# Gate sums and the first value projections as 128-column matmuls, and two admission settings of the planner, in a two-branch attention kernel

## The chip, the cores and the metric

The kernel runs on one core of a Trainium2 chip. The metric is the device time of one execution in microseconds (us). Lower is better. Four runs of the kernel before are given, and their median is what a changed kernel is compared with.

## The reference, cut to what matters

The input x has 2048 rows (tokens) of 512 features. Everything is in bf16 at the interface.

```python
g = sigmoid((x * gate_w).sum(-1, keepdims=True))      # one number per token
a = full attention of x, 32 heads of 16, then @ A_wo  # softmax(q k^T / 4) v
b = windowed attention of x: each token sees itself and 7 earlier ones,
    two apart, 32 heads of 16, then @ B_wo
return g * a + (1 - g) * b
```

The full attention (branch A) is by far the larger part: 32 heads times 2048 x 2048 scores have to be exponentiated. Branch B has only eight scores for each token and head.

## The kernel before, in words

**Units.** The scores of branch A are made in units. A unit is one head, 128 keys (the partitions) and 512 queries (the free axis). Four heads make a group (`NG` = 8 groups), 512 queries a chunk (`NC` = 4 chunks), and one pair of chunk and group is a *period*: 32 periods of 4 x 16 = 64 units, 2048 units in all. Four heads lie in four 32-row strips of the TensorE array, so several score matmuls (`kt_all` as weights, `qt` streaming) can run at the same time.

**Three ways for a unit to be exponentiated.** Most units are written into two PSUM rings, A with three banks and B with two. ScalarE (ACT) reads a whole ring with one activation (`pT<-ring`, 128x1536 or 128x1024) while TensorE fills the other ring. Other units go to a spare PSUM bank (`w0` or `w1`). From there VectorE (DVE) computes the exponential as a cubic in four passes (`ta`, `ta`, `ta`, `pd`), or GpSimd (POOL) does so after a copy (`psc`). Such a unit is called a rider when it is issued beside a ring fill. The result of each unit is multiplied by the values (`vp_all` as weights, 17 columns: 16 values and a one that sums the denominators) into one accumulator bank, `acc`.

**The other work** goes through the same two spare banks `w0` and `w1`, as *jobs*: the projections of keys (`k_job`, `kpk_job`), queries (`q_job`, `qpk_job`) and values (`v_job`, `v_group`), the gate sums (`g_job`), the transposes after each period (`post_job`, `ot_job`), branch B (`b_proj`, `b_attn`, most of it on POOL), and the output projections (`final_job`, two blocks of four matmuls).

**Order.** A planner (class `Plan`, lines 52 to 289) decides at build time in which order each engine gets its instructions. It keeps an assumed duration for each step and a list of ready steps for each engine. The hardware then executes each engine's list in that order and waits on semaphores where data is missing. The parts of it that the change touches:

- `fits` (line 216) lets a job with priority 2 or more onto PE only if it ends before ACT would run out of work. The tolerated overrun grows by `RAMP` (line 182) for each microsecond that the job has waited beyond `CALM` = 4.
- `JW` (line 190) is used twice. In `room_for_job` (line 200) a job that needs a spare bank is admitted once DVE's planned backlog is at least `JW`, or after it has waited `JP` = 3. In `rider` (line 1068) a further rider is refused if DVE's backlog is at least `JW` and a job waits for a bank.
- `have` and `idle_fill` (lines 144 to 168) count how much of the last 3.4133 us PE streamed, and put filler matmuls (`z32` as weights, results that are zero) where that falls under a share of 0.80. `P.thin` tells the count how much of a step's assumed duration is not streaming.

**The places of the change.** `gw` (line 365) holds the gate vector as four columns. `g_job` (lines 781 to 805) makes for each of 16 token tiles one column of 16 sums, by four matmuls with one streamed column each, in four steps of 16 matmuls. `v_group(0, 4, ...)` (line 1577) makes the values of the first four heads, needed by the first period: eight token tiles share a bank, 64 columns each. `v_group(4, 8, ...)` (line 1584) makes those of the next four heads for the third period. `v_group(8, 16, ...)` makes eight heads at a time with four token tiles in a bank, so 128 columns each.

## Time and profile before

| What | Value |
|---|---|
| Median of 4 runs | 860.02 us (855.65, 859.66, 860.39, 861.17) |
| The profiled execution | 860.39 us, of which span of instructions 858.6 us |
| ACT busy | 832.5 us (97%) |
| PE busy | 758.6 us (88%) |
| DVE busy | 749.5 us (87%) |
| POOL busy | 735.1 us (86%) |
| Mean granted TensorE clock | 0.983 |
| First and last `pT` activation | starts at 18.67 us, ends at 849.15 us |

The profile is one execution. "Busy" is the time in which an engine had at least one instruction in work, and matmuls are pipelined, so a busy PE is not PE at its peak. A *group* is all instructions of the same engine, operation and tiles, with their count, total busy time and mean duration. A group's durations can add up to more than its busy time, since neighbouring activations or matmuls overlap. The *timeline* lists instructions in order of time, merged where nothing came between, with the idle time of the engine before them in brackets and what ended it. In the *windows* view each line is a stretch of time with every engine's busy time and the granted clock of TensorE. Nearly all instructions carry line 347, that of a helper, so tiles are used to tell them apart. A number of an activation in the order of rings (ring 0 is the first) is used for places: rings follow each other every 1.13 us or so.

### The profile page before, as it was taken

The page shows a single profiled execution, that of the slowest core. Times are in us where ns is not written, and L with a number is a line of the kernel's source. Part 1 is how long each engine was busy: PE and PEld are TensorE (multiplying, and loading weights), DVE is VectorE, ACT ScalarE, POOL GpSimd, SP SyncE. Part 2 cuts the span into 40 slices and gives each one's busy share as a digit, 9 for nine tenths or more (in the row PEclk, how much of TensorE's full clock was granted, in tenths as well). Part 3 has the DMA queues.
Part 4 walks back from the last instruction along what each step waited for, and adds up shares of the span by engine and source line. Part 5 has one row for each costly group of instructions (what it writes and reads, how often), then busy time and mean ns, then how long its engine had stood idle before and what let it go on. Part 6 is the DMA issues. An engine that isn't in the chain of part 4 may idle for free.

```text
span 858.6 us, 15867 instructions
## 1 busy us (share of the span) xinstructions
PE 758.6 (88%) x5935; PEld 268.7 (31%) x5935; DVE 749.5 (87%) x1314; ACT 832.5 (97%) x753; POOL 735.1 (86%) x740
## 2 busy tenths in 40 slices
PE   8999999888898898888889899988888989888897
PEld 4333343333233222323233233332322332222232
DVE  4488989899899889889999988899889998899896
ACT  4899999999999999999999999999999999999996
POOL 2576798999898999898999998989999998978871
PEclk9799999999999989999999999999999999799999
DMA  9001233412314231121030314213003203010000
GB/s 294 2 2 49 81 113 117 134 62 76 117 44 136 90 107 68 51 67 50 8 111 31 100 37 141 75 56 111 1 14 117 74 21 122 20 50 7 1 2 26
DMA packets 55727, 59.78 MB, mean 70 GB/s; under 512 B 3665, under 2 KB 52305, under 8 KB 55649
## 3 DMA queue, kind: packets, MB, share of 16 engines
q1 hardware_dynamic: 54304, 58.37, 21.2%
q8 instruction: 46, 0.75, 0.4%
q10 hardware_dynamic: 1344, 0.39, 0.2%
q14 instruction: 33, 0.26, 0.1%
HBM read 46.14 MB, written 12.62 MB: 68 GB/s over the span
## 4 chain that ended last, share of the span: by engine, by line
ACT 66%; issue 21%; PE 11%; DVE 1%; POOL 0%; ACTq 0%
ACT pT L347 65%; PE acc L347 4%; PE ring L347 3%; PE w L347 3%; ACT lg L347 1%; DVE ta L347 1%; PE s L347 1%; PE e L347 0%; POOL prod L347 0%; DVE absq L347 0%; DVE kpk L347 0%; POOL lg L347 0%; ACT osc L347 0%; DVE accS L347 0%; DVE pd L347 0%
## 5 line engine op out<-in xcount | busy, mean ns | idle before, releaser
L347 ACT ACTIVATE pT<-ring 128x1536 bf16<-128x1536 f32 x722 | 822.3, 1386 | 9.6 <-PE ring L347 5.6
L347 PE MATMUL ring<-qt,kt_all 32*128 32x512 bf16 x1849 | 290.3, 385 | 89.9 <-ACT pT L347 75.1
L347 DVE SCALAR_TENSOR_TENSOR ta<-ta,w 128x512 f32<-128x512 f32 x450 | 301.8, 682 | 6.5
L347 POOL TENSOR_TENSOR prod<-prod 128x512 f32<-128x512 f32 (+1 forms) x208 | 240.4, 1167 | 6.0
L347 PE MATMUL acc<-pT,vp_all 128*17 128x512 bf16 x1804 | 228.7, 388 | 3.0 <-DVE accS L347 2.2
L347 PEld LDWEIGHTS <-kt_all 32*128 32x128 bf16 x2093 | 112.4, 91 | 334.2 <-issue 317.2
L347 DVE TENSOR_SCALAR ta<-w 128x512 f32<-128x512 uint16 x225 | 153.4, 685 | 41.9 <-PE w L347 39.5
L347 PE MATMUL acc<-ident,z 128*17 128x512 bf16 (+5 forms) x660 | 166.2, 337 | 1.4 <-DVE wkp L347 1.4
L347 DVE SCALAR_TENSOR_TENSOR pd<-ta,w 128x512 uint16<-128x512 f32 x225 | 151.6, 677 | 1.8
L347 POOL TENSOR_TENSOR prod<-ksh,qb 128x512 f32<-128x512 bf16 x128 | 145.1, 1157 | 2.4
L347 POOL TENSOR_TENSOR prod<-vsh,lg 128x512 f32<-128x512 bf16 x128 | 136.7, 1099 | 2.5
L347 PE MATMUL w<-qt,kt_all 32*128 32x512 bf16 x244 | 93.2, 387 | 0.2 <-DVE pd L347 0.2
L347 PE MATMUL acc<-pd,vp_all 128*17 128x512 bf16 x244 | 80.1, 387 | 0.0
L347 PEld LDWEIGHTS <-vp_all 128*17 128x17 bf16 x2048 | 42.0, 88 | 98.1 <-issue 97.6
L347 POOL TENSOR_TENSOR psc<-psc 128x512 f32<-128x512 f32 x57 | 68.1, 1194 | 4.4
L347 PEld LDWEIGHTS <-z 128*17 128x17 bf16 (+1 forms) x666 | 46.4, 92 | 64.8 <-issue 44.8
L347 POOL TENSOR_SCALAR psc<-psc 128x512 f32<-128x512 uint16 (+1 forms) x38 | 23.6, 621 | 42.1 <-DVE psc L347 34.4
L347 PE MATMUL w<-bw,xT 128*128 128x512 bf16 x192 | 49.7, 381 | 0.3
L347 PEld LDWEIGHTS <-xT 128*128 128x128 bf16 x512 | 30.8, 98 | 30.0 <-issue 17.1
L347 POOL TENSOR_TENSOR lg<-lg,mx 128x256 f32<-128x256 f32 x16 | 10.1, 630 | 25.8 <-DVE mx L347 23.7
L347 DVE CAST kvs<-w 128x512 bf16<-128x512 f32 x32 | 21.8, 682 | 4.1 <-PE w L347 4.1
L347 DVE COPY accS<-acc 128x512 f32<-128x512 f32 (+1 forms) x32 | 21.6, 676 | 2.8 <-ACT accS L347 2.0
(112 smaller groups left out, 487.5 us busy)
## 6 DMA issues: line engine op xcount, KB each, us to landing
ksh<-kv_scr SPq DMA_DIRECT2D x16, 1024.0 KB
vsh<-kv_scr SPq DMA_DIRECT2D x16, 1024.0 KB
kv_scr<-kvs SPq DMA_DIRECT2D x16, 256.0 KB
kt_all<-k_scr SPq DMA_DIRECT2D x6, 512.0 KB
q_scr<-qpk SPq DMA_DIRECT2D x24, 128.0 KB
qt<-q_scr SPq DMA_DIRECT2D x24, 128.0 KB
out_dram<-osb SPq DMA_DIRECT2D x14, 128.0 KB
xr<-in_A_x_dram SPq DMA_DIRECT2D x3, 512.0 KB
```

The source lines that it names most:

```text
L347: return chain_on(self._key, f(*a, **k))
```

## The change

```diff
-    RAMP = 0.02
+    RAMP = 0.01
...
-    JW = 1.6
+    JW = 1.2
...
-    gw = const.tile([128, DC], BF16, name="gw")
+    gw = work.tile([128, DC, 128], BF16, name="gw", tag="qpk", bufs=2)
...
-    with nc.allow_non_contiguous_dma(reason="tiny gate vector load"):
-        A.dma_start(out=gw[:], in_=gate_w.rearrange("(c p) -> p c", p=128))
...
     V.memset(z32[:], 0.0)
+    V.memset(gw[:].rearrange("p c n -> p (c n)").bitcast(U32), 0)
     V.memset(warm[:], 0.0)
+    with nc.allow_non_contiguous_dma(reason="tiny gate vector load"):
+        A.dma_start(out=gw[:, :, 0], in_=gate_w.rearrange("(c p) -> p c", p=128))
     A.activation(out=warm[:], in_=warm[:], func=ACT.Exp)
...
-                    w.open(s, [128, NT])
+                    w.open(s, [128, NT + 127])
+                P.thin = 0.06
                 for t in range(t0, t0 + 4):
-                    P.thin = 0.65
                     for c in range(DC):
-                        mm(w.t[:, t:t + 1], xT[:, c, t * 128:(t + 1) * 128], gw[:, c:c + 1], c == 0, c == DC - 1)
+                        mm(w.t[:, t:t + 128], xT[:, c, t * 128:(t + 1) * 128], gw[:, c, :], c == 0, c == DC - 1)
...
-            yield ("pe", prio, 0.8, pe(t0)) + (("w",) if t0 == 0 else ())
+            yield ("pe", prio, 0.99, pe(t0)) + (("w",) if t0 == 0 else ())
...
-        yield ("act", -1, 0.3, lambda: A.activation(out=e1[:], in_=w.t[:], func=ACT.Exp, scale=-1.0))
+        yield ("act", -1, 0.3, lambda: A.activation(out=e1[:], in_=w.t[:, 0:NT], func=ACT.Exp, scale=-1.0))
...
-    v_group(0, 4, None, 3)
+    v_group(0, 8, None, 3)
...
-    v_group(4, 8, ev_start[0], due(2) + 0.1)
```

The gate vector is now the first of 128 columns, of which the other 127 are zero. The tile takes one of the two buffers of the tag `qpk` instead of its own, is cleared by VectorE, and is loaded by ScalarE's DMA queue after that. A gate matmul streams 128 columns and writes column t of the bank and zeros into the next 127, which the following tiles overwrite. The values of heads 0 to 7 are made together by what was already the path for eight heads: four passes of four token tiles, each of 16 matmuls with 128 columns, in place of two plus two passes of eight tiles with 64 columns. `RAMP` and `JW` change the planner's admission of jobs, and so the order of PE's and DVE's lists through the whole kernel.

## The prediction

> **What bounds the kernel now.** I read the page first: the engine line, the granted clock by slices, and the two largest groups with their shapes kept apart.

> ```profile
> PE 758.6 (88%) x5935; PEld 268.7 (31%) x5935; DVE 749.5 (87%) x1314; ACT 832.5 (97%) x753; POOL 735.1 (86%) x740
> ...
> PEclk9799999999999989999999999999999999799999
> ```
> ```profile
> L347 ACT ACTIVATE pT<-ring 128x1536 bf16<-128x1536 f32 x361 | 577.4, 1600 | 8.2 <-PE ring L347 5.6 <-PE w L347 1.7 <-PE acc L347 0.2
> L347 ACT ACTIVATE pT<-ring 128x1024 bf16<-128x1024 f32 x360 | 422.8, 1175 | 1.3 <-PE w L347 0.9
> ```

> ACT is the bound, nearly without a pause. The reader sees 361 activations of three units, 360 of two (and one of one unit), and 8.2 + 1.3 = 9.5 us of idle time before them. The 2nd, 15th and 35th of the 40 slices (21.5 us each) have a low clock. The undisturbed rate comes from the chain of waits:

> ```profile
> 134.30 1.24 ACT pT L347
> 135.54 0.10 issue
> 135.64 0.87 ACT pT L347
> 136.51 0.04 issue
> 136.56 1.25 ACT pT L347
> ```

> A pair (five units) takes 136.56 - 134.30 = 2.26 us. The two of a pair sum to 1.600 + 1.175, so 0.51 us of overlap per pair, 0.26 per activation, is lost as well wherever ACT has to pause. The floor of the stream is 361 x 2.26 = 815.9, plus 0.8 for the last single unit, plus branch B's 16 softmax activations at 0.30 each (143.33 to 143.63 in the timeline), 4.7: together 821.4 us. It really ran from 18.67 to 849.15, 830.5 us. So 9.1 us are stalls, and no reordering can win more. Where are they? The timeline of ACT shows most of the idle time in one place:

> ```profile
> 33.32 2.36 ACT L347 ACTIVATE pT<-ring 128x1536 bf16<-128x1536 f32 x2 [0.72 <-PE ring L347]
> 36.93 1.45 ACT L347 ACTIVATE pT<-ring 128x1536 bf16<-128x1536 f32 x1 [1.24 <-PE ring L347]
> ...
> 41.62 1.02 ACT L347 ACTIVATE pT<-ring 128x1024 bf16<-128x1024 f32 x1 [0.69 <-PE w L347]
> 42.82 2.36 ACT L347 ACTIVATE pT<-ring 128x1536 bf16<-128x1536 f32 x2 [0.17 <-PE ring L347]
> ...
> 672.52 15.93 ACT L347 ACTIVATE pT<-ring 128x1536 bf16<-128x1536 f32 x14 [0.49 <-PE w L347]
> ```

> The windows view says why. These are three stretches, cut where the clock changes:

> ```profile
> 30.94:41.18 10.24, 10.24 (x72) 2.63 (x71) 5.96 (x8) 7.92 (x8) 9.40 (x11) 0.50 0.00 0
> 310.83:317.66 6.83, 6.82 (x35) 2.06 (x35) 4.89 (x11) 6.24 (x7) 6.20 (x8) 0.50 0.75 230
> 740.91:751.15 10.24, 9.93 (x55) 2.13 (x54) 8.02 (x14) 9.01 (x9) 10.08 (x10) 0.50 0.05 14
> ```

> PE is busy all through and the clock is half (0.50). From the ends of the activations, twenty rings take 22.6 us undisturbed. Rings 2 to 22 took 26.7, so the first cold stretch cost 4.1; the twenty rings around the second lost 1.7, around the third 1.5. That is 7.3 of 9.1; of the rest, 0.6 is at 672.5. What runs just ahead of the first one:

> ```profile
> 25.28 0.52 PEld L347 LDWEIGHTS <-xT 128*128 128x128 bf16 x16 [0.23 <-issue]
> 25.29 0.64 PE L347 MATMUL w<-wv,xT 128*128 128x64 bf16 x16
> ...
> 27.54 0.47 PEld L347 LDWEIGHTS <-xT 128*128 128x128 bf16 x16 [0.23 <-issue]
> 27.54 0.55 PE L347 MATMUL w<-gw,xT 128*128 128x1 bf16 x16
> ```

> Sixteen gate matmuls occupy PE for 0.55 us and stream sixteen columns.

> [...] the cold stretches are 10.24, 6.83 and 10.24 us, 3, 2 and 3 times 3.41, at clock 0.50. [...] The trace has 5.1 / 128 = 40 ns for 64 columns and 4.2 / 64 = 66 ns for 128 (value groups), so I use these.

> **The change part by part.**

> *Gate sums.* 64 matmuls of one column become 64 of 128. A step of 16 goes from 0.55 to 16 x 0.066 = 1.05 us: +0.5, four times +2.0 on PE. In the order of the built instructions each step still stands behind the fill of ring 8, 10, 12 or 14, with 11 score and value matmuls in the pair. By columns that pair is 1.76 us of PE against ACT's 2.26, so 0.5 of cover is left; without cover it would be 2.0 us.

> *Values.* 128 matmuls of 64 columns (5.1) become 64 of 128 (4.2), and all now stand in the first seven rings: four steps of 1.05 instead of four of 0.64 there, +1.6 on PE, and none at rings 26 to 37. Cover: PE waited 0.77, 0.52, 0.33 and 0.42 for ACT at 20.17, 22.43, 24.96 and 27.22, each more than the 0.4 added or near it. Four evacuations of 0.69 on DVE as before, two of them earlier, where DVE is busy 0.69 of 5 us. Cost 0, or up to 0.3 if the cover misses.

> *Clear and load of the gate tile.* 128x256 words, half of the `wkp` clear of 0.48: 0.24 us on DVE. It stands ahead of `warm`, two more clears and constants; DVE then idles 4.57 us before 7.92. PE's start waits for the first clear, which stays first. On ACT's queue the gate load (0.55) now waits for the clear; behind it are the table load and `warm`, then 2.25 idle before 5.58. Cost 0; 0.3 without that idle time. The load lands long before 27 us, and the shared buffer is next wanted by `qpk` near ring 62.

> *The clock at the start.* From ring 3 to 15 each pair of rings now carries 1.76 us of columns in its 2.26 us; before, it was 1.2 to 1.6 at the value steps and 1.34 at the gate steps. (Rings 1 and 2 carry 2.44, which the 0.77 us of waiting covers.) I take it that the first cold stretch goes: -4.1, bounds -4.1 and 0.

> *The order elsewhere.* The order shows what does not change: ACT's activations, shape by shape; 225 units on DVE, 19 on POOL. So the floor of 821.4 stays. What changes is where PE gets crowded. In the order of before, two consecutive blocks of four output-projection matmuls fall into neighbouring ring slots twice (rings 566 and 599, 2.59 us of columns against 2.26). The first is the 0.49 pause at 672.5 (0.6 lost), the second lost 0.2. After, this stands at seven places: rings 398, 424, 554 (2.59, one behind the other as at 672.5: 0.6 each), 403 (0.2), and 364, 410, 694 (2.37; 0.2 each). New too is a pile at ring 73: a value step, ten value matmuls, fp32 transposes and filler, 3.11 us: 0.85 over, plus the lost overlap 0.26, 1.1. Sum 1.8 + 0.2 + 0.6 + 1.1 = 3.7, less 0.8: +2.9. Against it, four such blocks of key projections and branch B in the slots of rings 39 to 55 that cost about 0.2 each are thinned out: -0.8. Bounds of this part: -1 to +6.

> *The later cold stretches.* Both follow the thinnest stretches of the old order: four rings with 2.0 us of columns near ring 248 and 1.84 at 625. The new order's thinnest are 2.0 and 2.06, its first percentile 2.16 against 2.01, with 14 more 512-column fillers. But equally thin places in the old one (545, 673) stayed warm. I take one stretch instead of two: -1.6, bounds -3.2 to +3.2.

> *A query that comes late.* The keys of the second group move from rings 19 to 24 to rings 26 to 34, so the query of the third period is finished (`selk_all` matmul) at ring 42 instead of 34, and used at 44. Between them DVE, in order, may have a cubic's last pass (0.68) and must do the query's evacuation (0.74), about 1.6 with hand-offs, against 2.26. Queued behind a late one on PE is every ring fill, so ACT waits. 0 if DVE is on time, 1.0 if it is one pass behind: +0.4.

> *Sum*, against the profiled execution's 860.39: - 4.1 + 2.9 - 0.8 - 1.6 + 0.4 = 857.2. That execution stands 0.4 over the median, so I put 857.4.

> **The rivals.**

> *All cold stretches go and the crowded places cost little* (1.5 instead of 3.7). For it: fuller thin places. 860.4 - 4.1 - 3.2 - 0.8 + 0.7 = 853.0; with a little of the late query, 854.

> *The clock falls anyway*, at the start or once more later, since the condition is not understood: the 44% window at 153.8 (share of time with columns streaming) kept its clock and the 51% one at 27.5 lost it. Then a stretch of 3 to 4 us comes back: 861.

> *Crowding wins, slower.* Place: the seven projection pairs and ring 73. Price 0.6 to 0.75 seen at 672.5. It decides from 1.25 us each: 8 x 1.25 = 10, less the 0.8 of before and less 4.1 and 0.8 gained, +4.3. That needs cold clock under several of them, where 2.59 us become 5.2. Against it: at full clock each is over by 0.33. With 1.5 each it is +6.3, 866 to 867.

> **How the numbers follow.** A measurement of this kernel can hardly tell less than 0.5%, 4.3 us, from nothing: faster is below 855.7, slower above 864.3. The main case has 0.55 (855 to 860 as its own range; a seventh of it below 855.7: 0.08), the first rival 0.2 (nearly all faster), the second 0.14 (same), slower 0.11. So faster 0.27, same 0.62, slower 0.11. The range leaves one in ten on each side: 853 to 864.

> **What would show it right or wrong.** Clock 1.00 from 30 to 42 us and no ACT pause over 0.3 there; gate steps near 1.05 us; 722 activations at 2.26 per pair; pauses of about 0.5 near 477, 506 and 652 us (rings 398, 424, 554) and 1 us near 103. It is wrong if the clock is 0.50 at the start, if DVE or `qt` holds ACT near 69 us, or if the pair's period differs.

## The result and the profile after

| | median of the runs | range |
|---|---|---|
| before | 858.58 us (56 runs) | 852.47 to 862.32 |
| after | 858.36 us (35 runs) | 856.38 to 861.21 |
| ratio after / before | 1.0005 | 95% interval 0.9991 to 1.0018 |

No difference can be measured. The four runs of before that were shown first (860.02) were a little above the median of the larger set. Ratios and their intervals leave out an execution that is more than 1.5% above the fastest of its kernel; of all runs below that is one, of experiment 5 (962.02 us).

The page of the changed kernel, its engine line and the granted clock:

```profile
PE 748.0 (87%) x5902; PEld 271.6 (32%) x5902; DVE 749.9 (88%) x1315; ACT 831.1 (97%) x753; POOL 734.9 (86%) x740
...
PEclk9999999999999999999999999999999999999999
```

The two groups of activations, with their shapes apart (count, busy time and mean, then idle time before them by what ended it):

```profile
L347 ACT ACTIVATE pT<-ring 128x1536 bf16<-128x1536 f32 x361 | 587.4, 1627 | 6.4 <-PE ring L347 3.0 <-PE w L347 1.7 <-PE acc L347 1.5
L347 ACT ACTIVATE pT<-ring 128x1024 bf16<-128x1024 f32 x360 | 432.6, 1202 | 0.8 <-PE ring L347 0.7
```

ACT is still the bound, with the same 361 and 360 activations and a pair still at 2.26 us. Its idle time before them is 7.2 us, 9.5 before. The clock has no low slice left. The windows of after, first the whole stream and then the three stretches that were cold in before (time, busy time of PE, PEld, DVE, ACT, POOL with counts, clock, DMA share, GB/s):

```profile
7.31:853.81 846.50, 742.12 (x5886) 269.64 (x5885) 747.50 (x1299) 829.25 (x750) 729.52 (x727) 1.00 0.22 69
30.94:41.18 10.24, 10.10 (x98) 4.30 (x96) 8.09 (x14) 10.24 (x11) 9.40 (x11) 1.00 0.01 2
310.83:317.66 6.83, 5.57 (x52) 2.14 (x48) 5.86 (x14) 6.83 (x8) 6.21 (x8) 1.00 0.01 3
740.91:751.15 10.24, 8.59 (x73) 2.95 (x70) 10.01 (x16) 10.24 (x10) 10.08 (x10) 1.00 0.11 35
```

All four show clock 1.00, and ACT is busy 10.24 of 10.24 us where it had 7.92. So all three cold stretches are gone from the profiled execution, and yet its span is only 3.7 us shorter (854.9 against 858.6). The timeline of ACT in after shows what took their place (rows with a pause):

```profile
102.34 38.52 ACT L347 ACTIVATE pT<-ring 128x1536 bf16<-128x1536 f32 x34 [1.47 <-PE acc L347]
...
168.07 16.84 ACT L347 ACTIVATE pT<-ring 128x1024 bf16<-128x1024 f32 x15 [0.70 <-PE ring L347]
...
477.03 1.45 ACT L347 ACTIVATE pT<-ring 128x1536 bf16<-128x1536 f32 x1 [0.49 <-PE w L347]
...
482.35 9.14 ACT L347 ACTIVATE pT<-ring 128x1536 bf16<-128x1536 f32 x8 [0.40 <-PE w L347]
...
491.78 15.92 ACT L347 ACTIVATE pT<-ring 128x1536 bf16<-128x1536 f32 x14 [0.28 <-PE w L347]
...
508.20 11.40 ACT L347 ACTIVATE pT<-ring 128x1536 bf16<-128x1536 f32 x10 [0.49 <-PE w L347]
...
656.88 28.78 ACT L347 ACTIVATE pT<-ring 128x1536 bf16<-128x1536 f32 x25 [0.49 <-PE ring L347]
```

One more, of 0.28, is at 816.55. These are pauses at full clock, most of them in places where PE has more to do than ACT's period allows. Before had one such pause over 0.25 us within the stream (at 672.52), apart from those in or just behind a cold stretch. The balance of the two profiled executions, from the ends of the activations by stretches of twenty rings, is this: -7.3 us for the cold stretches (4.1 + 1.7 + 1.5), and +3.6 for pauses at full clock (6.4 us of losses after against 10.1 - 7.3 = 2.8 before). Together that is -3.7, the difference of the spans.

**Why the medians agree all the same.** Each execution lists its mean granted clock, and within a kernel the time follows it closely. A straight line through all runs of a kernel, time against clock, falls by 4.1 us (before) and 4.7 us (after) per 0.01, and gives the time at clock 1.00:

| kernel | mean clock of the runs | mean time | time at clock 1.00 by the line | lost to the clock |
|---|---|---|---|---|
| before (its runs beside experiments 1 to 4) | 0.988 | 858.1 | 853.1 | 5.0 |
| after | 0.995 | 858.5 | 856.1 | 2.4 |

Scatter about the lines is 0.9 and 0.5 us. Both lines are carried by runs near their end: at a mean clock of 0.997 or more the median of before is 853.2 (8 runs), that of after 856.6 (7 runs). So the change halves what the clock costs (-2.6) and adds 3.0 us of pauses at full clock.

### The profile page after: what moved, and what is told of

Same layout as the page of the kernel before. It is cut to its first block, busy times and chain, and to the rows that moved or that the text cites. A ratio compares the mean times of both kernels' runs of the same rounds, so it can differ in the third digit from the quotient of the medians.

```text
span 854.9 us, 15807 instructions
## 1 busy us (share of the span) xinstructions
PE 748.0 (87%) x5902; PEld 271.6 (32%) x5902; DVE 749.9 (88%) x1315; ACT 831.1 (97%) x753; POOL 734.9 (86%) x740
## 4 chain that ended last, share of the span: by engine, by line
ACT 68%; issue 19%; PE 9%; DVE 3%; POOL 0%; ACTq 0%; POOLq 0%
ACT pT L347 67%; PE w L347 3%; PE acc L347 2%; PE ring L347 2%; DVE ta L347 2%; PE s L347 1%; ACT lg L347 1%; PE e L347 0%; DVE pd L347 0%; DVE kvs L347 0%; POOL prod L347 0%; DVE mx L347 0%; DVE mbias L347 0%; DVE crow L347 0%; DVE osb L347 0%
## 5 line engine op out<-in xcount | busy, mean ns | idle before, releaser
L347 ACT ACTIVATE pT<-ring 128x1536 bf16<-128x1536 f32 x722 | 821.3, 1414 | 7.2 <-PE ring L347 3.7
L347 PE MATMUL ring<-qt,kt_all 32*128 32x512 bf16 x1858 | 287.6, 380 | 95.3 <-ACT pT L347 79.4
L347 DVE SCALAR_TENSOR_TENSOR ta<-ta,w 128x512 f32<-128x512 f32 x450 | 302.6, 681 | 6.7
L347 POOL TENSOR_TENSOR prod<-prod 128x512 f32<-128x512 f32 (+1 forms) x208 | 240.3, 1168 | 5.9
L347 PE MATMUL acc<-pT,vp_all 128*17 128x512 bf16 x1804 | 223.6, 383 | 3.7 <-DVE accS L347 3.4
L347 PEld LDWEIGHTS <-kt_all 32*128 32x128 bf16 x2102 | 115.1, 91 | 335.9 <-issue 318.3
L347 DVE TENSOR_SCALAR ta<-w 128x512 f32<-128x512 uint16 x225 | 153.8, 685 | 47.0 <-PE w L347 45.2
L347 PE MATMUL acc<-ident,z 128*17 128x512 bf16 (+5 forms) x685 | 167.2, 330 | 1.4 <-POOL ident masks.py:199 1.4
L347 DVE SCALAR_TENSOR_TENSOR pd<-ta,w 128x512 uint16<-128x512 f32 x225 | 152.0, 678 | 2.4
L347 POOL TENSOR_TENSOR prod<-ksh,qb 128x512 f32<-128x512 bf16 x128 | 145.3, 1158 | 2.2
L347 POOL TENSOR_TENSOR prod<-vsh,lg 128x512 f32<-128x512 bf16 x128 | 136.8, 1101 | 2.5
L347 PE MATMUL w<-qt,kt_all 32*128 32x512 bf16 x244 | 91.5, 383 | 0.0
L347 PE MATMUL acc<-pd,vp_all 128*17 128x512 bf16 x244 | 80.1, 381 | 0.0
L347 PEld LDWEIGHTS <-vp_all 128*17 128x17 bf16 x2048 | 41.7, 87 | 95.6 <-issue 95.0
L347 POOL TENSOR_TENSOR psc<-psc 128x512 f32<-128x512 f32 x57 | 68.1, 1195 | 4.4
L347 PEld LDWEIGHTS <-z 128*17 128x17 bf16 (+1 forms) x688 | 46.8, 92 | 61.6 <-issue 39.0
L347 POOL TENSOR_SCALAR psc<-psc 128x512 f32<-128x512 uint16 (+1 forms) x38 | 23.6, 621 | 36.5 <-DVE psc L347 34.1
L347 PE MATMUL w<-bw,xT 128*128 128x512 bf16 x192 | 49.7, 381 | 1.2 <-DVE pd L347 1.1
L347 PEld LDWEIGHTS <-xT 128*128 128x128 bf16 x448 | 31.6, 98 | 28.8 <-issue 16.2
L347 POOL TENSOR_TENSOR lg<-lg,mx 128x256 f32<-128x256 f32 x16 | 10.1, 631 | 25.5 <-DVE mx L347 25.3
L347 DVE COPY accS<-acc 128x512 f32<-128x512 f32 (+1 forms) x32 | 21.5, 673 | 5.1 <-ACT accS L347 4.3
L347 DVE CAST kvs<-w 128x512 bf16<-128x512 f32 x32 | 21.8, 681 | 1.2 <-PE w L347 1.1
```

Source lines behind the costliest of these rows:

```text
L347: return chain_on(self._key, f(*a, **k))
```

## The experiments

There are five questions. Do the gate steps cool the clock, and how much is that worth (1, 2, 8)? Do the crowded places cost what was said (3)? Do the falls of TensorE's clock go with the rows of the array in work (5)? Does more filler help (6, 10)? And which part of the change gives the gain back (4, 7, 9, 11, 12)? The ratio is always to runs of before on the same chip. The last column but one is the line's time at clock 1.00, as above; it reaches beyond the runs for kernels whose clock was never above 0.996 (1, 7, 9, 11), and is rough there. The runs were made on several chips, and before itself has 852.7 to 853.5 at clock 1.00 on them.

| run | kernel | median us | ratio (95%) | at clock 1.00 | mean clock |
|---|---|---|---|---|---|
| 1 | after, gate streams one column | 860.22 | 1.0026 (1.0010 to 1.0042) | 855.6 | 0.990 |
| 2 | before, gate at 128 columns, plan as before | 857.98 | 0.9998 (0.9976 to 1.0020) | 854.7 | 0.991 |
| 3 | after, second projection block under the admission rule | 859.32 | 1.0013 (0.9993 to 1.0033) | 855.1 | 0.990 |
| 4 | after, old `RAMP` and `JW` (gate and values alone) | 860.95 | 1.0033 (1.0017 to 1.0049) | 858.7 | 0.994 |
| 5 | after, filler on 32 rows | 954.13 | 1.1072 (1.1011 to 1.1132) | | 0.840 |
| 6 | 3 with more filler | 855.95 | 0.9965 (0.9951 to 0.9979) | 854.1 | 0.997 |
| 7 | before, both settings | 862.17 | 1.0052 (1.0031 to 1.0073) | 855.1 | 0.988 |
| 8 | before, gate part with its plan | 855.24 | 0.9958 (0.9941 to 0.9975) | 852.5 | 0.993 |
| 9 | 8 and both settings | 861.79 | 1.0052 (1.0033 to 1.0071) | 856.7 | 0.990 |
| 10 | 8 with the edits of 6 | 858.70 | 1.0007 (0.9988 to 1.0027) | 856.4 | 0.996 |
| 11 | 8 and `RAMP` alone | 861.96 | 1.0060 (1.0035 to 1.0084) | 858.1 | 0.990 |
| 12 | 8 and `JW` alone | 855.57 | 0.9976 (0.9960 to 0.9992) | 853.8 | 0.996 |

### 1. The gate matmuls stream one column again

```diff
-                        mm(w.t[:, t:t + 128], xT[:, c, t * 128:(t + 1) * 128], gw[:, c, :], c == 0, c == DC - 1)
+                        mm(w.t[:, t:t + 1], xT[:, c, t * 128:(t + 1) * 128], gw[:, c, 0:1], c == 0, c == DC - 1)
```

Everything else, the order of all instructions included, is that of after.

> The changed kernel with its whole order and its assumed durations kept; only each gate matmul streams one column again instead of 128 (the values still in 128-column passes). Theory (the thin gate steps are what cools the clock): the clock falls to 0.50 within 31 to 38 us for two or three windows of 3.41 us, ACT pauses two or more times between 31 and 46 us, and rings 2 to 22 take 25 to 27 us instead of 22.7; the fastest runs 859 to 861, the median 2 to 4 us over the changed kernel's 858.4. Rival (the 64-column value passes cooled it, and these are gone): clock 1.00 to 45 us, time as the changed kernel, 856.4 to 858.5.

Measured: 860.22 us. In the profiled execution the cold stretch at the start is back (a second fall, of 3.41 us, is at 183.31), and the timeline has the short gate steps just ahead of it. That it isn't one odd execution is seen from the mean clocks: none of the 22 runs is above 0.995, while 7 of the 35 of after have 0.997 or more. The window of this run, cut where the clock is low, and the gate steps ahead of it:

```profile
29.71:39.95 10.24, 10.02 (x77) 2.61 (x75) 5.87 (x10) 9.08 (x9) 9.40 (x11) 0.50 0.00 0
```
```profile
26.67 0.55 PE L347 MATMUL w<-gw,xT 128*128 128x1 bf16 x16
...
28.93 0.55 PE L347 MATMUL w<-gw,xT 128*128 128x1 bf16 x16
```

In after those rows are

```profile
27.40 1.07 PE L347 MATMUL w<-gw,xT 128*128 128x128 bf16 x16
...
29.66 1.07 PE L347 MATMUL w<-gw,xT 128*128 128x128 bf16 x16
```

With two steps of 0.55 us and 16 streamed columns in each, the clock of this run fell to 0.50 at 29.71 us. With steps of 1.07 us and 2048 columns, that of after stayed at 1.00. Busy time does not tell the two apart. Here are the 3.41 us just ahead of the fall in before, and as long a stretch of after at the same place, where the clock stays:

```profile
27.53:30.94 3.41, 3.37 (x50) 1.67 (x47) 0.69 (x1) 3.41 (x4) 0.88 (x2) 1.00 0.02 5
```
```profile
28.00:31.41 3.41, 3.40 (x44) 1.77 (x41) 0.97 (x2) 3.41 (x4) 1.66 (x2) 1.00 0.02 5
```

PE is busy for 3.37 us of the one and 3.40 of the other. Only the loss in run 1 has another size than in before: rings 2 to 22 lost 2.3 us here, 4.1 there. Perhaps the pairs around the gate steps carry less other work here that a slow PE could be late with; this was not measured.

### 2. The 128-column gate in before, with the old plan

The gate tile, its clear and load, and the matmuls of after; the assumed 0.8 us and `P.thin` = 0.65 per tile of before.

> The kernel before with only the gate matmuls widened to 128 columns (with the clear and the later load of the gate tile), its order and assumed durations kept, values still in 64-column passes. Theory: no cold stretch at 31 us, rings 2 to 22 take 22.6 to 23.5 us; the later cold stretches come and go as before; median 1 to 4 us under the kernel before (855 to 857.5), fastest runs near 852.5 as before. Rival (64-column values alone cool the clock, or the fall has another cause): clock 0.50 near 31 us in the profile and a median as before, 858 to 859.

Measured: 857.98 us, not the gain that was expected. There is no cold stretch at the start (clock 1.00 to 309.7 us), but rings 2 to 22 still lost 2.1 us. The timeline of this run, rows of PE and ACT:

```profile
30.06 1.07 PE L347 MATMUL w<-gw,xT 128*128 128x128 bf16 x16
30.23 2.37 ACT L347 ACTIVATE pT<-ring 128x1536 bf16<-128x1536 f32 x2 [0.19 <-PE ring L347]
...
31.38 0.39 PE L347 MATMUL acc<-ident,z 128*17 128x512 bf16 x1
...
32.87 1.07 PE L347 MATMUL w<-gw,xT 128*128 128x128 bf16 x16
33.05 2.37 ACT L347 ACTIVATE pT<-ring 128x1536 bf16<-128x1536 f32 x2 [0.45 <-PE ring L347]
```

The planner still believed the gate step to be thin and put filler (`acc<-ident,z`) beside it. The pair now takes 32.87 - 30.06 = 2.81 us of PE against ACT's 2.26, where its streamed columns alone (2048 of the gate and six groups of 512, at 0.213 us per 512) would be 2.13. So the wide gate needs its new entry in the plan (0.99 us, `thin` 0.06): in run 8, with it, the filler beside the gate steps is gone, the steps follow each other every 2.26 us (26.60, 28.86, 31.12) and the twenty rings take 23.2 instead of 24.7.

### 3. The second projection block under the admission rule

```diff
-            yield ("pe", GO if a else prio, (b - a) * MM + SW, pe(a, b)) + (("w",) if a == 0 else ())
+            yield ("pe", 2.0 if a else prio, (b - a) * MM + SW, pe(a, b)) + (("w",) if a == 0 else ())
```

In `final_job` of after, the second block of four matmuls has the priority `GO`, which `fits` lets pass unseen; here it has to fit.

> The changed kernel, but the second block of four of each output projection has priority 2.0 instead of 1.9, so that it too must fit before ACT runs out of work. In the order this removes all seven neighbouring pairs of blocks (no two neighbouring rings over 2.3 us of columns after ring 73); one unit more is left to ACT (+0.45 us). Theory (those pairs are what the changed kernel loses after ring 100): the pauses near 438, 477, 482, 492, 508, 657 and 817 us are gone, 3 us less: fastest runs 853.5 to 854.5, median 855 to 856. Rival (the work only piles up elsewhere, or 7000 fewer filler columns let the clock fall more often): median 857.5 to 860.

Measured: 859.32 us, where the rival said 857.5 to 860. The pauses at 477, 482, 491 and 656 us are gone, and with them 0.6 to 0.9 us per twenty rings from ring 382 to 422 and at 542. (Around ring 422, where after pauses at 508.20, 0.6 is still lost, with a pause of 0.27 at 504.79.) But the clock falls instead, in three places where the profiled execution of after kept it (windows of this run):

```profile
165.88:169.29 3.41, 3.19 (x15) 0.64 (x14) 1.74 (x3) 1.59 (x2) 2.94 (x3) 0.50 0.46 148
722.25:732.49 10.24, 9.93 (x52) 2.38 (x51) 6.83 (x15) 9.12 (x9) 7.57 (x9) 0.50 0.20 58
773.45:780.28 6.83, 6.80 (x35) 1.78 (x32) 5.82 (x12) 5.51 (x6) 6.75 (x7) 0.50 0.00 0
```

So the crowded pairs cost about what the prediction said, up to 0.6 each, and removing them alone wins nothing, since the clock falls more often (mean 0.990 against 0.995). A likely reason is that this order streams 3% less filler (252 against 259 thousand columns in the two traces) and so has more thin stretches. Run 6 fits that, with a mean clock of 0.997, but it was not shown by itself.

### 4. Gate and values without the settings

After with `RAMP` = 0.02 and `JW` = 1.6.

> The changed kernel with the two admission settings as before (0.02 and 1.6): gate sums and values changed, nothing else. Its order has a heavier start of the key jobs (ring 19, 2.59 us) and ten crowded pairs after ring 300 instead of seven, but no pile at ring 72 to 73 (2.4 us at ring 95 instead of 3.1), and one unit fewer on ACT. Theory: clock 1.00 from 30 to 42 us all the same; the pile's 1.6 us at 103 gone, 3 to 4 us of crowded pairs; median 856 to 859, no clear difference from the changed kernel. Rival (the two settings carry the effect): cold stretch at 31 us again, median 860 or more.

Measured: 860.95 us, slower than before and than the 856 to 859 expected. In the profiled execution the activations end at 844.1 us, 1.5 earlier than in after, but the span ends at 856.7, 1.8 later. The end of this run in the timeline:

```profile
845.75 1.46 PE L347 MATMUL e<-bwo,obt 128*128 128x512 bf16 x6
847.13 0.38 PE L347 MATMUL acc<-pd,vp_all 128*17 128x512 bf16 x1
...
847.55 0.37 ACT L347 COPY accS<-acc 128x256 f32<-128x256 f32 x1 [3.49 <-PE acc L347]
```

The value matmul of the last GpSimd unit (`acc<-pd`) stands behind eleven projection matmuls in PE's order, and ACT waits 3.49 us for the accumulator. In after that matmul comes at 845.66, ahead of them, and the tail is 9.3 us instead of 12.6. Together with the values the new settings are therefore a gain (from 1.0033 to 1.0005), in the profiles chiefly by the order at the end.

### 5. Do the falls go with the rows in work?

```diff
-            mm(acc_tiles[p][32 * j:32 * j + DH + 1, 0:m], z32[:, 0:DH + 1], filling(m), False, False, tile_position=(0, 32 * j))
+            mm(acc_tiles[p][32 * j:32 * j + DH + 1, 0:m], z32[0:32, 0:DH + 1], filling(m)[0:32], False, False, tile_position=(0, 32 * j))
```

The filler in the stream uses 32 rows of the array instead of 128, for as many columns, at the same places. It adds zero in both. If the falls go with the rows in work (A), there have to be many more of them; if they go with the time in which columns stream (B) or with the number of instructions (C), no more than in after.

> The changed kernel with its order, its column counts and its number of instructions kept; only the filler matmuls into the accumulator take 32 rows of zeros instead of 128 (they add zero either way). In the six traces so far the windows of 3.41 us just ahead of a fall of the clock are those with the smallest share of array rows in work (mean over the window of rows streaming / 128: 0.30 to 0.38), while the share of time with any column streaming does not sort them. Theory A [...]: the clock falls many times, mean clock under 0.95, time over 863, up to 880. Theory B [...]: clock and time as the changed kernel, 856.4 to 861. Theory C [...]: as B.

Measured: 954.13 us (four runs, 943.31 to 962.02), 11% slower and far beyond the 880 that was named. The page is that of the longest run:

```profile
PE 921.0 (96%) x5902; PEld 265.9 (28%) x5902; DVE 755.6 (79%) x1315; ACT 846.5 (88%) x753; POOL 734.7 (77%) x740
...
PEclk9997998899786969799979997578999866555676
```

PE is busy for 96% of the span, and the clock is low for 331 us. The first fall is at 75.32 us. The 3.41 us ahead of it in this run,

```profile
71.91:75.32 3.41, 2.66 (x19) 0.97 (x18) 3.41 (x8) 3.41 (x4) 3.16 (x4) 1.00 0.15 41
```

and the same time in after, which kept its clock (the same instructions run there about 0.1 us later):

```profile
71.91:75.32 3.41, 2.67 (x22) 0.97 (x18) 3.41 (x8) 3.41 (x4) 3.16 (x4) 1.00 0.14 41
```

PE's busy time is the same to 0.01 us. Only the rows of the filler differ. An estimate from the two traces sets this in numbers. It counts 128 rows as in work at each moment in which a matmul of 128 rows streams, else 32 for each matmul of 32 rows that streams, and takes 0.213 us for 512 columns, as in the `w<-bw` row near the end. Columns stream in 0.53 of this window in both runs, but the mean share of rows in work is 0.32 in run 5 and 0.43 in after. So neither busy time nor the time with columns streaming tells these two windows apart, and the rows in work do. The stretch of 3.41 us is as long as the shortest falls within the stream (runs 1, 3, 6 and 11); the others that are named here last 6.83, 10.24 or 13.65 us, 2, 3 or 4 times as long.

### 6. More filler on top of 3

```diff
-    THIN = 0.40
+    THIN = 0.50
```

`THIN` (line 478 of after) is the share of the last 3.41 us with streaming work under which the planner adds a filler pass to a ring fill.

> The changed kernel with the second block of each output projection held to what fits (as in e3) and with a filler pass whenever PE streamed less than 0.50 of the last 3.41 us instead of 0.40 (THIN). Order: 722 activations, no neighbouring rings over 2.4 us of columns after ring 73; the smallest share of rows over three rings is 0.44, 0.46, 0.50 against 0.42, 0.43 in e3. Theory (e3 lost its gain to falls of the clock[...]): hardly any cold stretch, ACT stalls of 4 us, fastest runs 853.5 to 854.5, median 854 to 856, faster than both kernels. Rival (filler costs as much as it saves, or falls go on): median 857.5 to 860.

Measured: 855.95 us, ratio 0.9965, quicker than both kernels, as was expected. The profiled execution has one fall in the stream (592.58, 3.41 us), and no pause of ACT at the projection pairs. The pile at 101 us stays (ACT pauses 1.47), and two pauses of 0.48 and 0.47 at 148.9 and 150.4 are new.

### 7. The settings alone in before

```diff
-    RAMP = 0.02
+    RAMP = 0.01
...
-    JW = 1.6
+    JW = 1.2
```

> The kernel before with RAMP 0.01 and JW 1.2, nothing else. Its order leaves one activation and three units more to ACT (+1.4 us), has crowded places at rings 44 to 46 and 66 and four pairs later, and six thin places in rows (0.378 to 0.396) like the kernel before (five). Theory (the settings by themselves bring nothing; the gate steps still cool the clock at the start): cold stretch near 31 us in most runs, median 860 to 863. Rival (the settings are what evens out the falls): median 857 to 858.5, fewer runs over 860 than the kernel before.

Measured: 862.17 us, 0.5% slower, as the theory said. In the profiled execution the first cold stretch is longer (29.93 to 43.58) and rings 2 to 22 lose 5.3 us, so this run left two readings: the settings cost by themselves, or only through the clock. Run 9 decides between them.

### 8. The gate part with its plan

Before with all edits to `gw` and `g_job`, the assumed 0.99 us and `P.thin` = 0.06 included; the values and both settings as in before. The order is that of before, but for four fillers beside the gate steps that are no longer there, and one just after them that is longer.

> The kernel before with the gate sums alone as in the changed kernel, and the planner told of them (0.99 assumed for a step, thin 0.06). Its order differs from that of e2 in one thing: the four filler matmuls beside the gate steps are gone (3 us of PE columns less are not needed, the gate steps stream themselves); values, settings and the later order as before, with two thin places in rows later (0.378, 0.400). Theory (e2 lost 2.1 us at rings 2 to 22 because the filler stayed beside the wide gate matmuls): clock 1.00 to 45 us and rings 2 to 22 in 22.7 to 23.5 us; median 855.5 to 857.5, at or under the changed kernel. Rival (the pairs stay crowded, or the clock falls later as often): rings 2 to 22 over 24 us, median 858 to 859.

Measured: 855.24 us, ratio 0.9958, the lowest of all, though the intervals of runs 6 and 12 overlap with its own. The start keeps its clock, and rings 2 to 22 lose 0.6. What is left are two later falls, which cost 2.9 and 3.2 us of the profiled execution (its windows):

```profile
305.50:315.74 10.24, 9.89 (x46) 2.61 (x47) 7.25 (x16) 8.75 (x9) 8.88 (x11) 0.50 0.56 182
489.82:500.06 10.24, 9.82 (x49) 2.42 (x51) 6.60 (x14) 7.69 (x8) 10.08 (x10) 0.50 0.16 53
```

### 9, 11 and 12. Which setting gives the gain back

Run 9 is run 8 with both settings, 11 with `RAMP` = 0.01 alone, 12 with `JW` = 1.2 alone.

> The kernel before with the whole gate part (128 columns, 0.99 us in the plan) and RAMP .01, JW 1.2; values as before. Theory S (the two settings cost by themselves, wherever the clock is): the order has 723 activations (about 0.9 more) and seven places where the fill is over ACT's 2.26 us, so it gives back most of the 4 us that the gate part alone gained: 858 to 860. Rival C (the settings alone were slow only because their clock fell at the start for 13.65 us and cost 5.3): with the gate part in, nothing falls there, and it stands at 855 to 856.

> The gate part with its plan and RAMP .01 alone. Theory S (each setting makes crowded places of its own, and these can be counted in the order): three early places over ACT's 2.26 us at rings 44, 45 and 66, which took about 2.9 us together where both settings were in, and six pairs of projection blocks at 0.6, against one or two such pairs with the gate part alone: about 5.5 more than its 855.2, 859.5 to 862. Rival N (only the two settings together hurt, or the slot rule is worth nothing by itself): 855 to 857.

> The gate part with its plan and JW 1.2 alone. Theory S: no early place, four pairs of projection blocks at 0.6 and two at 0.2 that the gate part alone does not have: about 2.8 more than its 855.2, 857 to 859. Rival N: 855 to 856.5.

Measured: 861.79, 861.96 and 855.57 us. With both, the start keeps its clock and the kernel is as slow as in run 7 (and slower than the 858 to 860 expected), so the settings cost by themselves. It is `RAMP`: alone it takes the whole gain and more (1.0060), while `JW` alone can't be told from run 8 (0.9976 against 0.9958, intervals overlapping). The six crowded pairs expected of `JW` were to cost 2.8 us. The line's time at clock 1.00 is 1.3 above that of run 8, and the clock gives that back (0.996 against 0.993). So a count of such pairs in the order was too dear a price for `JW`. For `RAMP` it was right: 859.5 to 862 was expected of run 11.

Part of what `RAMP` does is in the timeline of run 11 around 70 us (the rows of one chain):

```profile
68.26 1.04 PE L347 MATMUL w<-xT,wqp 128*128 128x512 bf16 x4
...
69.34 0.69 DVE L347 TENSOR_SCALAR absq<-w 128x512 int16<-128x512 int16 x1 [1.96 <-PE w L347]
...
70.08 0.39 PE L347 MATMUL w<-absq,selk_all 128*128 128x512 bf16 x1
...
70.51 0.75 DVE L347 TENSOR_SCALAR qt<-w,qbias 128x512 bf16<-128x512 f32 x1 [0.48 <-PE w L347]
...
71.43 0.39 PE L347 MATMUL ring<-qt,kt_all 32*128 32x512 bf16 x3
...
71.96 1.45 ACT L347 ACTIVATE pT<-ring 128x1536 bf16<-128x1536 f32 x1 [0.90 <-PE w L347]
```

The projection of a query (`wqp`) comes just before its period; with the smaller `RAMP` it waits longer for a slot that fits. Then projection, `absq`, `selk_all`, `qt` and the ring fill run one behind the other in 3.2 us, and ACT pauses 0.90. The same chain comes once more at 94.75, and ACT pauses 1.10 at 98.38. Runs 7 and 9, which have the same `RAMP` and the old values, show the same two pauses (0.90 and 1.10, 0.89 and 1.10). In after the chain for the first of these is done at 67.1 us (`qt` at 66.33, 0.75 long) and ACT does not pause there. After differs from run 9 in the values alone, so it is the moved values that spare it this. That they leave the room for the query is likely, and was only argued. Later in run 11, pairs of projection blocks pause ACT by 0.49 to 0.51 at 432.5, 462.8, 488.3, 507.2 and 698.4; at 0.6 each that is 3 us, more than the two early pauses.

Run 11 shows one thing more. The clock of its profiled execution is low from 21.74 to 25.15 us, before any gate step, and rings 2 to 22 lost 1.1. The 3.41 us ahead of that fall hold two value steps of 64 columns, and the estimate of experiment 5 gives 0.35 of the rows for them. So with the old values the start can still lose its clock under the wide gate, though among six such profiles (2, 8, 9, 10, 11, 12) only this one did.

**The values by themselves.** Run 4 differs from run 8 in the values alone, and there the values cost 0.75% (1.0033 against 0.9958). About half of it is the end: 12.6 us from the last activation, 9.5 in run 8. After differs from run 9 in the values alone too, and there they gain 0.5% (1.0005 against 1.0052). So either of the two, the values or `RAMP`, takes more than the whole gain of the gate part when it stands alone with it; together they take 0.5%.

### 10. The edits of 6 on the gate part

> The kernel before with the whole gate part, the second block of an output projection under the admission rule, and the filler's fill-up factor 0.50; values and settings as before. Theory: the gate part alone had two later falls that cost 2.9 and 3.2 us; with more filler (243 riders, 722 activations) at least one of them goes: 851 to 854. Rival (the filler itself crowds PE, at three places near rings 68, 78 and 126, with 0.6 to 1.3 each): 855 to 857, no better than the gate part alone at 855.2.

Measured: 858.70 us, no better than before and outside the 851 to 854 expected. Its clock is good (0.996, one fall of 3.41 us in the stream of the profiled execution), but the time at clock 1.00 is 856.4, 3.9 above run 8: ACT pauses 0.52, 0.52, 0.53, 0.43, 0.48, 0.55 and 0.50 us at 98.5, 102.8, 111.1, 147.2, 152.3, 153.9 and 168.0. The rival was right in kind (PE gets crowded) and too cheap; whether it is the filler or the admission rule that crowds it here was not taken apart. No version beats run 8.

## Why the prediction was right, and where it was not

The forecast of no clear difference was right, and the median (857.4 forecast, 858.36 measured) was near. There was luck in it. The forecast was a gain of 2.6 us on the 860.02 of four runs; measured is a gain of 0.2 on 858.58. The sum for the profiled executions came close by two misses against each other: -7.3 for the clock where the steps had -4.1 - 1.6 = -5.7, and +3.6 for the order where they had 2.9 - 0.8 + 0.4 = +2.5; so -3.7 against -3.2.

- *The floor and the unchanged count.* Right: 361 and 360 activations, 2.26 us a pair. The stream went from 830.5 to 826.8 us (18.80 to 845.61), so the stalls from 9.1 to 5.4.
- *Gate step 0.55 to 1.05 us, hidden.* Right: 1.07, and ACT has no pause over 0.25 us from the first activation to 102 us. The prediction's 66 ns for a matmul of 128 columns are a step's length shared out, with the end of its last matmul in it. In a gate step of after the matmuls start 57 ns apart. The length of the step came out the same. The cover as worked out, "By columns that pair is 1.76 us of PE against ACT's 2.26", was too generous. Run 2 shows a pair of 2.13 us by columns that takes 2.81. A group of 512 columns with 32-row or 17-column tiles, such as three score matmuls that take 0.39 us together and 0.38 each, has the next group start 0.31 to 0.33 us later, while 512 columns within a chain take 0.213 ((1.02 - 0.38) / 3 in the `w<-bw` row below), so each change of group is worth about 0.1 us that columns do not show, an estimate.
- *The first cold stretch goes, -4.1.* Right in mechanism, shown by run 1. The size is that of one execution: it was 2.3 in run 1 and 5.3 in run 7. Nor does every execution of before have it: the fastest have a mean clock of 0.998 to 1.000, which leaves no room for 10.24 us at half clock.
- *The later cold stretches, -1.6.* A step whose working did not hold. It compared streamed columns, and in run 5 the mean clock went from 0.995 to 0.840 with the columns unchanged and fewer rows in the filler. In the profiled execution both went. Over the runs the clock still costs after 2.4 us, before 5.0. So the gain by the clock was -7.3 in one profile and -2.6 on average: the profiled execution of before had more falls than its mean run, that of after fewer.
- *Crowded places, 0.6 and 0.2 each.* The places were right (477, 508 and 656 us were named as 477, 506 and 652), and so was the 0.6. The seven pairs and smaller ones near them cost 3.5 where the sum had 2.6. Against it, the blocks of rings 39 to 55, thinned out for -0.8, gave about half: rings 22 to 62 lost 1.0 in before and 0.5 after.
- *The pile at ring 73, 1.1.* It cost 1.6, and by another wait. The timeline of after:

```profile
99.99 0.39 PE L347 MATMUL ring<-qt,kt_all 32*128 32x512 bf16 x3
...
100.32 1.07 PE L347 MATMUL w<-wv,xT 128*128 128x128 bf16 x16
...
101.32 0.39 PE L347 MATMUL ring<-qt,kt_all 32*128 32x512 bf16 x2
...
101.64 0.82 PE L347 MATMUL acc<-pT,vp_all 128*17 128x512 bf16 x9
```

  The ring was filled by 101.7, but the pause that ends at 102.34 is ended by `acc`: the activation needed a `pT` buffer, and the nine value matmuls that free it stood behind the value step. The prediction counted only the ring fill.
- *Unforeseen: 0.8 at 168 us.* Again the timeline of after:

```profile
163.76 1.02 DVE L347 TENSOR_TENSOR mbias<-cneg,m 128x1 f32<-128x1 f32 x1
...
166.62 1.02 PE L347 MATMUL w<-bw,xT 128*128 128x512 bf16 x4 [1.07 <-DVE pd L347]
```

  A branch-B projection waited 1.07 us for a spare bank that a late cubic still held, and everything behind it on PE with it. The cubic was late behind `mbias`, a DVE step of one column that took 1.02 us here and 0.14 and 0.15 the other two times; why it took so long is open. The order shows where PE has too much to do, but not where it waits for DVE.
- *A late query, +0.4.* It did not come in after (0), and came twice where `RAMP` was smaller and the values old (runs 7, 9 and 11, 0.9 and 1.1). The mechanism was real, its cause misplaced: it came with the smaller `RAMP`, and only where the values were the old ones.
- *The rivals.* "All cold stretches go" came true in the profiled execution without its time (853 to 854), because the crowded places cost far more than its 1.5 (3.5 at the pairs and 1.6 at the pile). "The clock falls anyway" is what the runs at 860.8 to 861.2 show, with a mean clock of 0.990. "Crowding wins" needed 1.25 us per place, and the pairs cost 0.6.

What the steps left out is that the parts of the change pull in different directions. The gate part with its plan is worth -0.4%. On top of it `RAMP` alone costs 1.0%, the values alone 0.75%, and values and settings together only 0.5%, which makes the zero. The prediction priced the settings and the values through one list of crowded places.

## What to carry to other kernels

Before a low clock is put down to an idle PE, look at how many rows of the array the matmuls ahead of the fall use and how few columns they stream: here the clock fell to 0.50 right behind 3.41 us of which PE was busy for 3.37 (before, from 27.53 us), with 0.37 of the rows in work by the estimate of experiment 5. The cheap cure was to widen that step and to tell the planner its new length. When an order has been planned close to the bound, price an admission rule by what becomes late under it (here a query's chain just before its use), not by its purpose, and try each part of a change by itself and with each other part: the gate part alone was better than the whole, and two parts that each cost alone cost less together. Compare profiled executions only together with the mean clock of many runs, since one profile can have more or fewer falls than is usual.
